# A one-core kernel with a long convolution and a gated MLP: the convolution traced one PSUM tile at a time, its taps on VectorE, its tap gradients as channel products on TensorE, weight tiles of 2 KB per partition

## The chip, the cores and the metric

The kernel runs on one core of one Trainium2 chip. Times are device microseconds (us) of that core, from the start of the program to its end. TensorE (PE) multiplies, VectorE (DVE), ScalarE (ACT) and GpSimd (POOL) do elementwise work, and SyncE (SP) issues the DMAs. Each engine takes its instructions strictly in the order in which they were put into its stream.

## The reference

One block is computed forwards and backwards (S = 2048 rows, D = 1024 channels, F = 3584, bf16 in and out). A small-tap convolution and a 2048-long one run along the rows, channel by channel, beside a gated MLP on the same normalised input:

```python
def _A_ref(q, k, v, shift_k, ssm_k, ssm_D):      # q is xn
    for t in range(4):
        k_shift = k_shift + k_pad[:, t:t + S, :] * shift_k[:, 3 - t][None, None, :]
    kv = k_shift * v
    y = irfft(rfft(kv, 2 * S) * rfft(ssm_k, 2 * S))[:S] + kv * ssm_D
    return q * y
def _B_ref(x, W_gate, W_up, W_down):             # x is xn
    gate = relu(x @ W_gate); h = gate * (x @ W_up)
    return h @ W_down
x = A_q
xn = _layernorm(x, axis=-1)
out = x + _A_ref(xn, A_k, A_v, ...) + _B_ref(xn, B_W_gate, B_W_up, B_W_down)
grads = vjp(...)(grad_out)   # of x, k, v, shift_k, ssm_k, ssm_D, W_gate, W_up, W_down
```

## The kernel before

**The MLP (branch B)** is a run of phases, nearly all of their work matmuls of 128x128 weights on 512 columns. `gate_up` takes 7 blocks `fb` of 512 features, in each 16 row tiles `st`; for one (fb, st) 8 matmuls fill the PSUM tile ps_g and 8 fill ps_u (L585). ACT then makes ru = relu(ps_g) (L600), DVE the gated ps_u (L601), POOL the product ht (L603), and SP stores both to DRAM (ru_d, h_d). `grad_hidden` has 8 matmuls into ps_h per (fb, st), loads ru back (rul), multiplies on DVE (L633) and stores ug_d. `grad_down` (ps_d) and `grad_in` (ps_w) are sums over 16 row tiles (L659), with slabs hs and ugs loaded from DRAM as the streamed operands. `out_phase` (ps_o, L742) and `grad_x` (ps_x, L775) come last. Each of the first four phases has 896 or 1792 such matmuls: gate_up 1792, grad_hidden 896, grad_down 896, grad_in 1792. Weights and slabs use one pool of 6 tiles of [128, 4, 512] (512 KB each).

**The convolution (branch A)** runs over 8 groups of 128 channels. One group is a chain: the small taps of k (`ksh`), the product with v, the transforms of h, g and kv as two matmul steps each (`fwd1`, `fwd2`) with a 32x32 transpose on DVE between them (`flip`, L301), three complex products on DVE (`cmul`: GKV, Y, GH), the inverses (`inv_a`, flip, `inv_b`), and the gradients (`gradients`: gv, gks, and gk by four taps of gks). A PSUM tile of A is 128 partitions by 1024 f32; there are two of them (`aps`), and ACT copies each out (L68). A tap is a POOL product of two halves of 128x1024 (L278) and, from the second tap on, a DVE addition (L72). The gradient of the taps multiplies gks with shifted kp on DVE (`pr`, four of 128x2048 per group) and sums over rows on PE with a selector matrix (`hsel`). Before the gradient taps are complete, gks needs three rows of halo, which come through a small DMA on itself (`gks<-gks`). The tap weights are spread over the partitions by a matmul (`shift_b`, ps_sk).

**What sets the order.** The kernel's Python is traced with priorities (`Pri`): MLP work and A's matmuls and loads are `now`, A's evacuations and stores `late`, and a scheduler lays each engine's instructions out by these. `mlp()` yields after each (fb, st) or 16-matmul sum the time that its matmuls take (3460 ns); when the sum of these has passed 55 us (`A_START`), A's generator `steps()` is advanced: every `yield` in it states how many ns of MLP work are to come before its next piece. A piece is a whole method: all 4 tiles of `fwd1` or of `inv_a`, or 4 tiles of `fwd2`.

Of the kernel before, what the change touches and what calls it, by code (L numbers as in the profile page):

```python
# [17 lines left out]
P = 128  # L18
# [24 lines left out]
class ABranch:  # L43
# [3 lines left out]
    def __init__(self, tc, pri, S, D, k, v, g, shift_k, ssm_k, ssm_D, xn_d, y_d, out_gk, out_gv, out_gsk, out_gh,  # L47
                 out_gsD):
# [54 lines left out]
    def tables(self):  # L103
# [103 lines left out]
        V.memset(self.ones[:], 1.0)  # L207
        V.memset(self.hsel[:], 0.0)
        for i in range(4):
            V.memset(self.hsel[:, i, i:i + 1], 1.0)  # L210
        make_identity(nc, self.identA[:])
        sk_b = con.tile([P, self.NG, 4], BF16, name="sk_b")
        nc.sync.dma_start(out=sk_b[:], in_=self.shift_k.rearrange("(g c) i -> c g i", c=P))
        V.tensor_copy(out=self.skf[:], in_=sk_b[:])
        row = self.ts.tile([1, self.D], BF16, name="sdrow", tag="ts")
        nc.sync.dma_start(out=row[0:1, :], in_=self.ssm_D.rearrange("(o d) -> o d", o=1))
        w = min(1024, self.D)
        psb = self.ps.tile([P, 1024], F32, name="psb", tag="aps")
        for c0 in range(0, w, 512):
            ce = min(w, c0 + 512)  # L220
            nc.tensor.matmul(psb[:, c0:ce], lhsT=self.ones[0:1, :], rhs=row[0:1, c0:ce], start=True, stop=True)
        nc.scalar.copy(out=self.sDb[:], in_=psb[:, 0:w])
# [21 lines left out]
    def loads_2(self, st):  # L244
# [9 lines left out]
        st["kp"], st["vt"] = kp, vt  # L254

    def shift_b(self, st):
        gi = st["gi"]
        dg = self.tmp.tile([P, 4, P], BF16, name="dg", tag="tmp")
        for i in range(4):
            self.pri.late()  # L260
            self.nc.vector.tensor_scalar(out=dg[:, i, :], in0=self.identA[:], scalar1=self.skf[:, gi, i:i + 1],
                                         scalar2=None, op0=ALU.mult)
        ps = self.ps.tile([P, 1024], F32, name="ps_sk", tag="aps")
        self.mm(ps[:, 0:512], self.ones[:], dg[:].rearrange("p i c -> p (i c)"))
        skb = self.sm.tile([P, 4, 1, P], BF16, name="skb")
        self.act(skb[:].rearrange("p i o c -> p (i o c)"), ps[:, 0:512])
        st["skb"] = skb

    def taps(self, st, out, src, offs):

        skb = st["skb"]
        for n, (i, off) in enumerate(offs):
            for hf in range(2):
                rows = slice(off + 8 * hf, off + 8 * hf + 8)
                o = out[:, 8 * hf:8 * hf + 8, :]
                t = o if n == 0 else self.tap.tile([P, 8, P], BF16, name="tap", tag="tap")[:]
                self.pri.late()
# [26 lines left out]
    def fwd1(self, src):  # L304
# [10 lines left out]
        return self.flip(B)  # L315

    def fwd2(self, Bf, form_name, add_D=None):
        F = self.frm.tile([P, 2, 16, P], BF16, name=form_name, tag="frm")
        for k0 in range(0, NB1, 8):
# [5 lines left out]
            re, im = F[rows, 0, kl:kl + 8, :], F[rows, 1, kl:kl + 8, :]  # L325
# [5 lines left out]
        return F  # L331

# [17 lines left out]
    def inv_a(self, Q):  # L350
# [6 lines left out]
        return self.flip(C)  # L357

    def inv_b(self, Cf, dst):
        for j in range(2):  # L360
# [6 lines left out]
            self.act(dst[:, 8 * j:8 * j + 8, :].rearrange("p r c -> p (r c)"), ps[:])  # L367

    def inv_b_chan(self, Cf, dst):
        dv = dst[:, 0:16, :].rearrange("p r c -> p (r c)").rearrange("p (q n) -> p n q", n=NB1)  # L370
        for n0 in range(0, NB1, 16):
# [3 lines left out]
            self.act(dv[:, n0:n0 + 16, :], ps[:])  # L375

    def steps(self):


        nc, pri = self.nc, self.pri  # L380
        nx = self.loads_1(0)
        self.loads_2(nx)
        for gi in range(self.NG):
            st, nx = nx, None
            cg, kp, vt, gt = st["cg"], st["kp"], st["vt"], st["gt"]
            self.shift_b(st)
            hT = self.h_tile(st)
            ksh = self.lng.tile([P, 16, P], BF16, name="ksh")
# [3 lines left out]
            yield 7000  # L392
            Hf = self.fwd1(hT)
            yield 8000
            Gf = self.fwd1(gt)
            yield 8000
            H = self.fwd2(Hf, "H", add_D=self.sDb[:, cg].rearrange("p (o c) -> p o c", o=1))
            if gi + 1 < self.NG:
                nx = self.loads_1(gi + 1)
            yield 8000  # L400
            Kf = self.fwd1(kvt)
            yield 8000
            G = self.fwd2(Gf, "G")
            GKV = self.cmul(H, G, True, "GKV")
            yield 8000
            K = self.fwd2(Kf, "K")
            Y = self.cmul(H, K, False, "Y")
            yield 12000
            Cg = self.inv_a(GKV)
            yield 9000  # L410
            Cy = self.inv_a(Y)
            GH = self.cmul(K, G, True, "GH")
            yield 8000
            gkv = self.ttile("gkv")
            self.inv_b(Cg, gkv)
# [5 lines left out]
            yield 8000
            Ch = self.inv_a(GH)
            yield 5000
            ps = self.ps.tile([P, 1024], F32, name="ps6", tag="aps")
            for i in range(4):
                pr = self.tmp.tile([P, 16, P], BF16, name="pr", tag="tmp")
                self.tt(pr[:], gks[:, 0:16, :], kp[:, 3 - i:19 - i, :], ALU.mult)
                yield 3500
                for j in range(4):
                    self.mm(ps[:, 0:512], self.hsel[:, i, :], pr[:, 4 * j:4 * j + 4, :].rearrange("p r c -> p (r c)"),  # L430
                            start=(i == 0 and j == 0), stop=(i == 3 and j == 3))
            gsf = self.sm.tile([4, P], F32, name="gsf", bufs=1)
            pri.late()
            nc.vector.tensor_reduce(out=gsf[:], in_=ps[0:4, 0:512].rearrange("p (r c) -> p c r", r=4), axis=AX.X,
                                    op=ALU.add)
            self.vcopy(self.gs_all[:, gi, :], gsf[:])
# [25 lines left out]
    def small_outputs(self):  # L462
        nc, NG = self.nc, self.NG
        tp = nc.tensor.transpose
        ps = self.ps.tile([P, 1024], BF16, name="ps7", tag="aps")
        for g in range(NG):
            self.pri.now()
            tp(ps[:, 4 * g:4 * g + 4], self.gs_all[:, g, :], self.identA[0:4, 0:4])
# [17 lines left out]
class LnMlp:  # L486
# [7 lines left out]
    def open_left(self):  # L494
# [18 lines left out]
    def w_tile(self, name):  # L513
        return self.w4.tile([P, 4, 512], BF16, name=name, tag="w4")
# [9 lines left out]

    def layer_norm(self, x, xn_d, xpool, xtag, jpool, jtag, spool):
# [3 lines left out]
        for n in (1, 1, 2, 4, 4, 4):  # L529
            xt = xpool.tile([P, 4, D], BF16, name="ln_x", tag=xtag)  # L530
            nc.sync.dma_start(out=xt[:, 0:n, :], in_=x[st0 * P:(st0 + n) * P, :].rearrange("(t p) d -> p t d", p=P))
# [28 lines left out]
            for j in range(n):  # L560
# [3 lines left out]
                nc.sync.dma_start(out=xn_d[st * P:(st + 1) * P, :], in_=xt[:, j, :])  # L564
# [336 lines left out]
```

## Time and profile before

| | |
|---|---|
| Time, median of 3 runs | 2415.14 us (2412.49 to 2415.37) |
| The profiled execution | 2409.23 us, of which span 2407.4 us |
| PE busy | 2053.3 us, 85% of the span (mean granted clock 0.948) |
| DVE, ACT, POOL busy | 1136.8 us (47%), 722.2 us (30%), 463.1 us (19%) |
| DMA | 352.52 MB, mean 146 GB/s |

A row of a group of waits states for whom an engine stood idle, how long in total, how many times, and the longest. A row of a timeline states start, duration, the instruction with its output and inputs, and in brackets the idle time ahead of it and what ended it. The granted clock is a share of TensorE's full speed. The phases follow one another on PE: first matmul of gate_up at 57.4 us, of grad_hidden at 641.6, of grad_down at 968.7, of grad_in at 1336.0, of out_phase at 1811.6; the last instruction ends at 2407.4.

### The profile page before, as it was taken

What the parts mean: (1) busy time and instruction counts of PE and PEld (TensorE: products, weight loads), DVE (VectorE), ACT (ScalarE), POOL (GpSimd) and SP (SyncE); (2) the same over time, 40 slices, a digit from 0 to 9 for tenths busy, and PEclk for the clock granted to TensorE, in tenths of its full rate; (3) what the DMA queues carried; (4) which work ended last, traced back from release to release, by engine and by line L of the source; (5) the groups of instructions that cost most, each with busy time, mean ns of one, the idle gap of its engine ahead of it and who ended that gap; (6) DMA issues with size and microseconds to landing.
All of it is one profiled execution on the core that took longest, in us unless ns stands there. A gap on an engine that the chain in (4) does not pass through costs nothing.

```text
span 2407.4 us, 26357 instructions
## 1 busy us (share of the span) xinstructions
PE 2053.3 (85%) x10379; PEld 969.4 (40%) x10583; DVE 1136.8 (47%) x1445; ACT 722.2 (30%) x880; POOL 463.1 (19%) x270
## 2 busy tenths in 40 slices
PE   2988689789778858787969688999999899999998
PEld 2434334334334423343424334444444344444443
DVE  6568558557667835386856437300001122232323
ACT  6335335145246422455536236311110000000000
POOL 0342552552530122014150320300000000000000
PEclk9999899899889979898989899999999999999999
DMA  7333433445579867642333521493329975454542
GB/s 232 127 118 108 131 122 110 132 123 145 144 222 271 244 176 242 197 112 73 114 96 120 147 81 62 142 308 109 105 88 220 265 186 138 103 138 101 138 101 70
DMA packets 591166, 352.52 MB, mean 146 GB/s; under 512 B 410817, under 2 KB 530625, under 8 KB 591042
## 3 DMA queue, kind: packets, MB, share of 16 engines
q1 hardware_dynamic: 591042, 350.83, 51.8%
q8 instruction: 83, 1.36, 0.2%
q14 instruction: 41, 0.34, 0.0%
HBM read 154.93 MB, written 124.79 MB: 116 GB/s over the span
## 4 chain that ended last, share of the span: by engine, by line
PE 38%; DVE 8%; DMA 6%; SPq 3%; issue 2%; ACT 2%; POOL 2%; DVEq 0%; ACTq 0%; POOLq 0%
PE ps_x L775 16%; PE ps_w L659 11%; PE ps_o L742 6%; PE ps_d L659 3%; DMA ugs<-ug_d 2%; DVE t L72 2%; DVE flp L301 2%; POOL tap L278 2%; PE ps L64 1%; SPq L734 1%; DVE ksh L72 1%; DVE Y L72 1%; DMA hs<-h_d 1%; ACT G L68 1%; DMA gks<-gks 1%
## 5 line engine op out<-in xcount | busy, mean ns | idle before, releaser
L659 PE MATMUL ps_w<-ugs,xn_nat 128*128 128x512 bf16 x1752 | 401.1, 383 | 20.9 <-DMA ugs<-ug_d 16.5
L585 PE MATMUL ps_u<-wu,xnT 128*128 128x512 bf16 x881 | 230.8, 402 | 82.6 <-DVE ru L601 69.3
L585 PEld LDWEIGHTS <-xnT 128*128 128x128 bf16 x1792 | 177.5, 101 | 300.2 <-issue 115.7
L659 PEld LDWEIGHTS <-xn_nat 128*128 128x128 bf16 x1792 | 175.3, 99 | 233.6 <-issue 34.4
L659 PE MATMUL ps_d<-g_nat,hs 128*128 128x512 bf16 x867 | 222.2, 400 | 28.2 <-DMA hs<-h_d 18.5
L585 PE MATMUL ps_h<-wdT,goT 128*128 128x512 bf16 x872 | 212.4, 396 | 16.8 <-DVE ru L601 9.9
L585 PE MATMUL ps_g<-wg,xnT 128*128 128x512 bf16 x865 | 220.2, 386 | 2.4 <-ACT ru L600 0.5
L603 POOL TENSOR_TENSOR ht<-ru 128x512 bf16<-128x512 bf16 x112 | 151.6, 1358 | 364.0 <-DVE ru L601 274.8
L742 PE MATMUL ps_o<-wd,hT 128*128 128x512 bf16 x878 | 193.3, 379 | 7.6 <-DMA hT<-h_d 6.7
L775 PE MATMUL ps_x<-wuT,guT 128*128 128x512 bf16 x878 | 197.5, 379 | 0.9
L775 PE MATMUL ps_x<-wgT,ggT 128*128 128x512 bf16 x878 | 197.5, 379 | 0.9
L744 DVE TENSOR_TENSOR o<-ps_o,ya 128x512 bf16<-128x512 f32 x32 | 21.4, 687 | 302.4 <-PE ps_o L742 302.2
L695 ACT CAST wi<-ps_w 128x512 bf16<-128x512 f32 x112 | 65.8, 592 | 304.5 <-PE ps_w L659 257.9
L585 PEld LDWEIGHTS <-goT 128*128 128x128 bf16 x896 | 89.9, 101 | 147.1 <-issue 54.8
L600 ACT ACTIVATE ru<-ps_g 128x512 bf16<-128x512 f32 x112 | 68.1, 609 | 245.4 <-PE ps_g L585 159.0
L659 PEld LDWEIGHTS <-hs 128*128 128x128 bf16 x896 | 88.4, 102 | 130.7 <-DMA hs<-h_d 22.1
L633 DVE TENSOR_TENSOR rul<-rul,gh 128x1024 bf16<-128x1024 bf16 x112 | 94.7, 857 | 90.6 <-DMA rul<-ru_d 61.8
L742 PEld LDWEIGHTS <-hT 128*128 128x128 bf16 x896 | 87.4, 98 | 113.3 <-DMA hT<-h_d 8.6
L775 PEld LDWEIGHTS <-guT 128*128 128x128 bf16 x896 | 87.7, 98 | 105.7
L775 PEld LDWEIGHTS <-ggT 128*128 128x128 bf16 x896 | 87.7, 98 | 105.7
L72 DVE TENSOR_TENSOR gk<-gk,tap 128x1024 bf16<-128x1024 bf16 x48 | 74.2, 1568 | 117.0 <-POOL tap L278 117.0
L777 DVE CUSTOM_DVE_ANT_0 gx<-ps_x,gy 128x512 f32<-128x512 f32 x32 | 22.1, 691 | 226.7 <-PE ps_x L775 216.1
(169 smaller groups left out, 2358.3 us busy)
## 6 DMA issues: line engine op xcount, KB each, us to landing
ru_d<-ru SPq DMA_DIRECT2D x112, 256.0 KB, 2.0
rul<-ru_d SPq DMA_DIRECT2D x112, 256.0 KB, 3.9
ug_d<-rul SPq DMA_DIRECT2D x112, 256.0 KB, 3.1
ugs<-ug_d SPq DMA_DIRECT2D x56, 512.0 KB, 5.8
h_d<-ht SPq DMA_DIRECT2D x112, 128.0 KB, 1.7
hs<-h_d SPq DMA_DIRECT2D x28, 512.0 KB, 5.1
out_dram<-wi SPq DMA_DIRECT2D x56, 256.0 KB, 5.4
wg<-in_B_W_gate_dram SPq DMA_DIRECT2D x14, 512.0 KB, 7.4
```

Source lines behind the costliest of these rows:

```text
L64: self.nc.tensor.matmul(out, lhsT=lhsT, rhs=rhs, start=start, stop=stop)
L72: self.nc.vector.tensor_tensor(out=out, in0=in0, in1=in1, op=op)
L278: self.nc.gpsimd.tensor_tensor(out=t, in0=src[:, rows, :], in1=skb[:, i, :, :].to_broadcast([P, 8, P]), op=ALU.mult)
L301: self.nc.vector.transpose(out=df[:, c0:c0 + 32, :], in_=sf[:, c0:c0 + 32, :])
L585: self.nc.tensor.matmul(ps[:], lhsT=xT[:, kt * P:(kt + 1) * P], rhs=w(kt), start=(kt == 0), stop=(kt == self.DT - 1))
L600: nc.scalar.activation(out=ru[:, 0, :], in_=ps_g[:], func=ACT.Relu)
L603: nc.gpsimd.tensor_tensor(out=ht[:], in0=ru[:, 0, :], in1=ru[:, 1, :], op=ALU.mult)
L633: nc.vector.tensor_tensor(out=ru[:], in0=ru[:], in1=gh[:].rearrange("p (o f) -> p o f", o=1).to_broadcast([P, 2, 512]), op=ALU.mult)
L659: self.nc.tensor.matmul(ps[:], lhsT=lhsT(st), rhs=rhs(st), start=(st == 0), stop=(st == self.ST - 1))
L695: nc.scalar.copy(out=wo[:, d, :], in_=ps[:])
L742: nc.tensor.matmul(ps[:], lhsT=hT[:, kt, :], rhs=self.wd[:, kt, oc], start=(kt == 0), stop=(kt == self.FT - 1))
L775: nc.tensor.matmul(ps[:], lhsT=T[:, kt, :], rhs=W[:, kt, oc], start=(i == 0), stop=(i == n - 1))
```

## The change

A's methods `fwd1`, `fwd2`, `inv_a`, `inv_b`, `inv_b_chan` become generators that yield after every PSUM tile, and the MLP yields after every 8 matmuls (1730 ns) where it yielded after 16. Each phase has a pace by which its ns count: 1.0, 0.72, 1.3, 1.3. The taps are DVE products of 128x2048 with the weight broadcast over 16 rows, and DVE additions of the same size; the product ht moves from POOL to DVE. The tap gradients are 16 matmuls gks[r] transposed times kp[r to r+3], 512 columns wide, summed in one PSUM tile, whose four diagonals DVE takes out (a product with the identity and a reduction). The tap weights come from DRAM by a broadcasting load, and `shift_b` goes. In `fwd2` of h ACT evacuates both halves, and D is added once, to 32 rows of the tile B. `inv_b_chan` writes its rows in another order. Weights and slabs become 13 tiles of [128, 2, 512] (256 KB each). In the layer norm all weights of the first block (2 MB) are issued right behind the first chunk of x, and the stores of xn go through POOL's queue.

```diff
     def taps(self, st, out, src, offs):
         skb = st["skb"]
         for n, (i, off) in enumerate(offs):
-            for hf in range(2):
...
-                self.nc.gpsimd.tensor_tensor(out=t, in0=src[:, rows, :], in1=skb[:, i, :, :].to_broadcast([P, 8, P]),
-                                             op=ALU.mult)
-                if n > 0:
-                    self.tt(o, o, t, ALU.add)
+            t = out if n == 0 else self.tmp.tile([P, 16, P], BF16, name="tap", tag="tmp")
+            self.tt(t[:, 0:16, :], src[:, off:off + 16, :], skb[:, i, :, :].to_broadcast([P, 16, P]), ALU.mult)
+            if n > 0:
+                self.tt(out[:, 0:16, :], out[:, 0:16, :], t[:, 0:16, :], ALU.add)
...
+    def grad_taps(self, gi, gks, kp, ns):
+        ps = self.ps.tile([P, 4, P], F32, name="ps6", tag="aps")
+        for r in range(16):
+            self.mm(ps[:].rearrange("p b c -> p (b c)"), gks[:, r, :], kp[:, r:r + 4, :].rearrange("p b c -> p (b c)"),
+                    start=(r == 0), stop=(r == 15))
+            if r % 4 == 3:
...
+                yield ns
...
-            if add_D is not None:
-                self.tt(re, ps[0:64], add_D[0:64].to_broadcast([64, 8, P]), ALU.add)
-            else:
-                self.act(re, ps[0:64])
-            self.act(im, ps[64:128])
+            self.act(F[rows, 0, kl:kl + 8, :], ps[0:64])
+            self.act(F[rows, 1, kl:kl + 8, :], ps[64:128])
+            yield ns
...
-            self.act(dv[:, n0:n0 + 16, :], ps[:])
+            self.act(dv[:, :, n0:n0 + 16], ps[:].rearrange("p n q -> p q n"))
+            yield ns
...
-        return self.w4.tile([P, 4, 512], BF16, name=name, tag="w4")
+        return self.w2.tile([P, 2, 512], BF16, name=name, tag="w2")
...
-                nc.sync.dma_start(out=xn_d[st * P:(st + 1) * P, :], in_=xt[:, j, :])
+                nc.gpsimd.dma_start(out=xn_d[st * P:(st + 1) * P, :], in_=xt[:, j, :])
...
-                nc.gpsimd.tensor_tensor(out=ht[:], in0=ru[:, 0, :], in1=ru[:, 1, :], op=ALU.mult)
+                nc.vector.tensor_tensor(out=ht[:], in0=ru[:, 0, :], in1=ru[:, 1, :], op=ALU.mult)
...
-                yield 3460
+                yield 1730
...
     pri.now()
+    b.ln_load(x, a.frm, "frm", 0)
+    first = b.gate_weights(B_W_gate, B_W_up, 0)
     b.layer_norm(x, xn_d, a.frm, "frm", a.tmp, "tmp", a.sm)
...
+        yield 1.0, b.gate_up(first, B_W_gate, B_W_up, ru_d, h_d)
+        yield 0.72, b.grad_hidden(B_W_down, g, ru_d, ug_d)
+        yield 1.3, b.grad_down(g, h_d, out_9)
+        yield 1.3, b.grad_in(xn_d, ug_d, out_7, out_8)
...
+            left -= ns * pace
```

How the streams move is seen at three places. The first is VectorE in gate_up, where the second group's gradient taps stand. Before, the taps' additions (gk<-gk,tap, in halves) are spread between ru's, each of them behind a POOL product:

```order
L72 TENSOR_TENSOR gks<-gkv,vt 128x2048
L72 TENSOR_TENSOR pr<-gks,kp 128x2048
L601 SCALAR_TENSOR_TENSOR ru<-ru,ps_u 128x512
L72 TENSOR_TENSOR pr<-gks,kp 128x2048
L72 TENSOR_TENSOR gk<-gk,tap 128x1024
L601 SCALAR_TENSOR_TENSOR ru<-ru,ps_u 128x512 x2
L72 TENSOR_TENSOR gk<-gk,tap 128x1024 x2
L601 SCALAR_TENSOR_TENSOR ru<-ru,ps_u 128x512
L72 TENSOR_TENSOR gk<-gk,tap 128x1024 x3
```

In the changed kernel the products stand on the same engine, and ht behind each ru (this is the first group's place):

```order
L72 TENSOR_TENSOR gv<-gkv,ksh 128x2048
L72 TENSOR_TENSOR gks<-gkv,vt 128x2048
L72 TENSOR_TENSOR gk<-gks,skb 128x2048
...
L606 TENSOR_TENSOR ht<-ru 128x512
L604 SCALAR_TENSOR_TENSOR ru<-ru,ps_u 128x512
L606 TENSOR_TENSOR ht<-ru 128x512
L72 TENSOR_TENSOR tap<-gks,skb 128x2048 x2
L72 TENSOR_TENSOR gk<-gk,tap 128x2048
L604 SCALAR_TENSOR_TENSOR ru<-ru,ps_u 128x512
L72 TENSOR_TENSOR gk<-gk,tap 128x2048
```

The `pr` products are gone, and a tap waits for no POOL product; its first product that needs the halo stands behind several ru's.

The second place is ScalarE at the first group's inverse transforms (C is what it copies from a PSUM tile of A). Before, four tiles stand together between ru's:

```order
L68 CAST C<-ps_1809 128x64x16
L68 CAST C<-ps_1819 128x64x16
L68 CAST C<-ps_1829 128x64x16
L68 CAST C<-ps_1839 128x64x16
L600 ACTIVATE ru<-ps_g 128x512 x3
```

After, a ru stands between every two, and PE has 8 MLP matmuls between the matmuls of one tile and of the next:

```order
L68 CAST C<-ps_1818 128x64x16
L68 CAST C<-ps_1843 128x64x16
L603 ACTIVATE ru<-ps_g 128x512
L68 CAST C<-ps_1863 128x64x16
L68 CAST C<-ps_1888 128x64x16
L603 ACTIVATE ru<-ps_g 128x512 x2
```

One tile of A per 8 matmuls of the MLP, where two were filled in a row.

The third place is SyncE around the halo DMA of the group that lies in grad_hidden. Before, it stands amid that phase's own loads and stores:

```order
L628 DMA rul<-ru_d 128x1024 x5
L636 DMA ug_d<-rul 256x1x512 x2
L84 DMA gks<-gks 127x384
L636 DMA ug_d<-rul 256x1x512
L628 DMA rul<-ru_d 128x1024 x2
```

After, it stands behind the whole phase and behind the first loads of the next:

```order
L639 DMA ug_d<-rul 256x1x512
L656 DMA g_nat<-in_grad_out_dram 128x1024 x10
L647 DMA hs<-h_d 128x2x512 x13
L84 DMA gks<-gks 127x384
L84 DMA y_d<-yt 2048x1x128
L683 DMA out_dram<-wo 128x1024
```

On PE this goes with a bare stretch: in the changed kernel A's tiles lie in the first 136 of the 896 ps_h matmuls, and 760 of them have no work of A between them. Counted on PE's stream, 2.74 groups of A then fall into gate_up, 3 into grad_down and 2 into grad_in, whose last 920 ps_w matmuls have none.

## Rows read from the trace of the kernel before

**Rows 1.** Windows by phase: PE, weight loads, DVE, ACT, POOL; clock, DMA, GB/s

```profile
57.40:641.60 584.20, 490.64 (x2589) 234.01 (x2638) 383.14 (x410) 233.18 (x270) 250.02 (x159) 0.94 0.42 125
641.60:968.70 327.10, 245.32 (x1235) 115.74 (x1258) 207.24 (x223) 129.75 (x166) 73.23 (x34) 0.89 0.78 227
968.70:1336.00 367.30, 299.55 (x1688) 146.24 (x1721) 245.90 (x238) 183.97 (x199) 80.55 (x38) 0.91 0.39 115
1336.00:1811.60 475.60, 425.19 (x2111) 197.76 (x2152) 108.02 (x106) 135.75 (x171) 55.30 (x26) 0.97 0.42 130
1811.60:2407.40 595.80, 578.26 (x2636) 262.64 (x2687) 157.54 (x332) 0.58 (x1) 0.00 (x0) 1.00 0.62 147
```

**Rows 2.** Waits of PE: for whom, us in total, times, longest

```profile
PE ps_u L585 <- DVE ru L601: 69.3, 21, 8.7
...
PE ps_d L659 <- DMA hs<-h_d: 18.5, 5, 10.7
PE ps_w L659 <- DMA ugs<-ug_d: 16.5, 13, 4.3
...
PE ps L64 <- ACT C L68: 11.2, 4, 6.5
...
PE ps_d L659 <- DMA g_nat<-in_grad_out_dram: 7.7, 1, 7.7
...
PE ps L64 <- ACT yt L68: 1.3, 3, 0.8
```

**Rows 3.** Waits of VectorE, same columns

```profile
DVE gk L72 <- POOL tap L278: 117.0, 25, 13.5
```

**Rows 4.** Waits of GpSimd, same columns

```profile
POOL tap L278 <- DMA gks<-gks: 70.8, 6, 26.9
```

**Rows 5.** Timeline of VectorE in gate_up, first group's gradient taps

```profile
261.84 3.19 DVE L72 TENSOR_TENSOR gk<-gk,tap 128x1024 bf16<-128x1024 bf16 x2 [10.36 <-POOL tap L278]
```

**Rows 6.** Timeline of PE at the same place

```profile
270.27 3.57 PE L585 MATMUL ps_u<-wu,xnT 128*128 128x512 bf16 x8 [8.60 <-DVE ru L601]
```

**Rows 7.** One window in grad_hidden, columns as in rows 1

```profile
880.00:895.00 15.00, 0.00 (x0) 0.00 (x0) 12.55 (x8) 4.17 (x2) 9.55 (x4) 0.50 0.38 122
```

**Rows 8.** Sum over windows 180 to 240, 360 to 420, 540 to 600

```profile
sum 180.00, PE 162.85 PEld 83.73 DVE 151.55 ACT 100.78 POOL 50.12; mean PE 54.28 PEld 27.91 DVE 50.52 ACT 33.59 POOL 16.71
```

**Rows 9.** One window of out_phase and grad_x, MLP matmuls alone

```profile
1980.00:2040.00 60.00, 59.68 (x274) 27.20 (x278) 12.67 (x25) 0.00 (x0) 0.00 (x0) 1.00 0.52 127
```

**Rows 10.** Timeline of PE: one tile of A's 128-column matmuls

```profile
184.47 0.61 PE L64 MATMUL ps<-flp,FW 128*128 128x128 bf16 x8
184.91 0.59 PE L585 MATMUL ps_u<-wu,xnT 128*128 128x512 bf16 x2
```

**Rows 11.** Line 72, VectorE by form: ns of one, minimum, median, maximum

```profile
L72 DVE TENSOR_TENSOR GKV<-t x64: 673/686/1550, 190.0 to 1472.4; 64x1024 bf16<-64x1024 bf16 x64
...
L72 DVE TENSOR_TENSOR ksh<-ksh,tap x48: 662/1635/2607, 124.3 to 1412.8; 128x1024 bf16<-128x1024 bf16 x48
...
L72 DVE TENSOR_TENSOR H<-ps,sDb x32: 1181/1217/1219, 158.8 to 1450.8; 64x1024 bf16<-64x1024 f32 x32
L72 DVE TENSOR_TENSOR pr<-gks,kp x32: 1199/1226/3149, 240.3 to 1544.9; 128x2048 bf16<-128x2048 bf16 x32
```

**Rows 12.** Line 68, ScalarE by form, same columns

```profile
L68 ACT CAST B<-ps x96: 1012/1018/1072, 125.6 to 1455.1; 128x1024 bf16<-128x1024 f32 x96
...
L68 ACT CAST ghn<-ps x16: 4612/4648/4993, 292.5 to 1556.5; 128x1024 bf16<-128x1024 f32 x16
```

**Rows 13.** Line 601, VectorE by form, same columns

```profile
L601 DVE SCALAR_TENSOR_TENSOR ru<-ru,ps_u x112: 651/680/690, 73.4 to 658.8; 128x512 bf16<-128x512 bf16 x112
```

**Rows 14.** Windows of ps_h's instructions: PE, ACT; granted clock, DMA share, GB/s

```profile
720.00:800.00 80.00, 60.25 (x259) 19.28 (x33) 0.98 0.98 273
937.00:962.00 25.00, 22.66 (x102) 9.36 (x16) 1.00 0.93 303
```

**Rows 15.** The page: what the DMAs moved, in 40 slices of the span

```profile
GB/s 232 127 118 108 131 122 110 132 123 145 144 222 271 244 176 242 197 112 73 114 96 120 147 81 62 142 308 109 105 88 220 265 186 138 103 138 101 138 101 70
```

More of the change, by code (lines that the diff above doesn't have):

```diff
@@ L205, in tables @@
                 V.tensor_scalar(out=o, in0=trB[:], scalar1=mh[:], scalar2=1.0 / 2048, op0=ALU.mult, op1=ALU.mult)
[L207 to L210, printed above, removed]
         make_identity(nc, self.identA[:])
[L212 to L222, printed above, removed]
+        sk_b = con.tile([P, self.NG * 4], BF16, name="sk_b")
+        nc.sync.dma_start(out=sk_b[:].rearrange("c (g i) -> c g i", i=4),
+                          in_=self.shift_k.rearrange("(g c) i -> c g i", c=P))
+        ps = self.ps.tile([self.NG * 4, P], BF16, name="ps_sk", tag="aps")
+        nc.tensor.transpose(ps[:], sk_b[:], self.identA[:])
+        sk_t = con.tile([self.NG * 4, P], BF16, name="sk_t")
+        V.tensor_copy(out=sk_t[:], in_=ps[:])
+        nc.sync.dma_start(out=self.sk_d, in_=sk_t[:])
+        nc.sync.dma_start(out=self.sDb[:], in_=self.ssm_D.partition_broadcast(P))
     def tview(self, ap2d, cg):
@@ L253, in loads_2 @@
         self.load(vt[:], self.tview(self.v, cg))
[L254 to L264, printed above, removed]
         skb = self.sm.tile([P, 4, 1, P], BF16, name="skb")
-        self.act(skb[:].rearrange("p i o c -> p (i o c)"), ps[:, 0:512])
-        st["skb"] = skb
+        self.load(skb[:].rearrange("p i o c -> p (i o c)"),
+                  self.sk_d[4 * st["gi"]:4 * st["gi"] + 4, :].rearrange("i c -> (i c)").partition_broadcast(P))
+        st["kp"], st["vt"], st["skb"] = kp, vt, skb
     def taps(self, st, out, src, offs):
@@ L385, in steps @@
             cg, kp, vt, gt = st["cg"], st["kp"], st["vt"], st["gt"]
-            self.shift_b(st)
             hT = self.h_tile(st)
+            yield 2000
+            yield from self.fwd1(hT, 2000, add_D=self.sDb[:, cg])
+            Hf = self.flipped
             ksh = self.lng.tile([P, 16, P], BF16, name="ksh")
@@ L416, in steps @@
             gks = self.gradients(st, gkv, ksh)
-            yield 8000
+            yield 6000
             yt = self.ttile("yt")
-            self.inv_b(Cy, yt)
+            yield from self.inv_b(Cy, yt, 2000)
             self.store(self.tview(self.y_d, cg), yt[:, 0:16, :])
[L421 to L436, printed above, removed]
+            yield from self.inv_a(GH, 1800)
+            Ch = self.flipped
+            yield from self.grad_taps(gi, gks, kp, 1800)
             if nx is not None:
                 self.loads_2(nx)
+            yield 1500
@@ L439, in steps @@
             ghn = self.ttile("ghn")
-            self.inv_b_chan(Ch, ghn)
+            yield from self.inv_b_chan(Ch, ghn, 2000)
             ghf = ghn[:, 0:16, :].rearrange("p r c -> p (r c)")
@@ L464, in small_outputs @@
         tp = nc.tensor.transpose
[L465 to L468, printed above, removed]
         sk = self.sm.tile([P, NG, 4], BF16, name="sk_o", bufs=1)
-        self.vcopy(sk[:].rearrange("p g i -> p (g i)"), ps[:, 0:4 * NG])
+        self.vcopy(sk[:], self.gs_all[:])
         ps = self.ps.tile([P, 1024], BF16, name="ps8", tag="aps")
@@ L523, in ps_tile, with ln_load @@
         return self.ps.tile([P, 512], F32, name=name, tag="bps")
+    LN_CHUNKS = (1, 1, 2, 4, 4, 4)
+    def ln_load(self, x, xpool, xtag, i):
+        if i >= len(self.LN_CHUNKS):
+            return
+        st0, n = sum(self.LN_CHUNKS[:i]), self.LN_CHUNKS[i]
+        xt = xpool.tile([P, 4, self.D], BF16, name="ln_x", tag=xtag)
+        self.nc.sync.dma_start(out=xt[:, 0:n, :], in_=x[st0 * P:(st0 + n) * P, :].rearrange("(t p) d -> p t d", p=P))
+        self.ln_x.append(xt)
     def layer_norm(self, x, xn_d, xpool, xtag, jpool, jtag, spool):
@@ L528, in layer_norm @@
         st0 = 0
-        for n in (1, 1, 2, 4, 4, 4):
-            xt = xpool.tile([P, 4, D], BF16, name="ln_x", tag=xtag)
-            nc.sync.dma_start(out=xt[:, 0:n, :], in_=x[st0 * P:(st0 + n) * P, :].rearrange("(t p) d -> p t d", p=P))
+        for i in range(1, 5):
+            self.ln_load(x, xpool, xtag, i)
+        for i, n in enumerate(self.LN_CHUNKS):
+            if i == 1:
+                self.ln_load(x, xpool, xtag, 5)
+            xt = self.ln_x[i]
             self.pri.now()
@@ L586, in gemm8, with gate_weights, gate_up @@
                                   stop=(kt == self.DT - 1))
-    def gate_up(self, Wg, Wu, ru_d, h_d):
+    def gate_weights(self, Wg, Wu, fb):
+        return self.col_block(Wg, fb, "wg"), self.col_block(Wu, fb, "wu")
+    def gate_up(self, first, Wg, Wu, ru_d, h_d):
         nc = self.nc
@@ L597, in gate_up @@
                 self.gemm8(ps_g, self.xnT[st], wg)
+                yield 1730
+                self.pri.now()
                 self.gemm8(ps_u, self.xnT[st], wu)
@@ L619, in grad_hidden @@
             wt = []
-            for q in range(2):
+            for q in range(4):
                 t = self.w_tile("wdT")
-                nc.sync.dma_start_transpose(out=t[:], in_=Wd[cols, q * 512:(q + 1) * 512])
+                nc.sync.dma_start_transpose(out=t[:], in_=Wd[cols, q * 256:(q + 1) * 256])
                 wt.append(t)
-            w = lambda kt: wt[kt // 4][:, kt % 4, :]
+            w = lambda kt: wt[kt // 2][:, kt % 2, :]
             for st in range(self.ST):
@@ L851, in mlp @@
     def mlp():
-        yield from b.gate_up(B_W_gate, B_W_up, ru_d, h_d)
-        yield from b.grad_hidden(B_W_down, g, ru_d, ug_d)
-        yield from b.grad_down(g, h_d, out_9)
-        yield from b.grad_in(xn_d, ug_d, out_7, out_8)
+        yield 1.0, b.gate_up(first, B_W_gate, B_W_up, ru_d, h_d)
+        yield 0.72, b.grad_hidden(B_W_down, g, ru_d, ug_d)
+        yield 1.3, b.grad_down(g, h_d, out_9)
+        yield 1.3, b.grad_in(xn_d, ug_d, out_7, out_8)
     a_steps, left = a.steps(), A_START
-    for ns in mlp():
-        left -= ns
-        while a_steps is not None and left <= 0:
-            d = next(a_steps, None)
-            if d is None:
-                a.close()
-                a_steps = None
-                b.open_right(B_W_down)
-            else:
-                left += d
+    for pace, phase in mlp():
+        for ns in phase:
+            left -= ns * pace
+            while a_steps is not None and left <= 0:
+                d = next(a_steps, None)
+                if d is None:
+                    a.close()
+                    a_steps = None
+                    b.open_right(B_W_down)
+                else:
+                    left += d
     b.close_left()
```

124 lines of the change are left out of this document (67 added, 57 removed).

## The prediction

> **What bounds the kernel now.** I read the windows by phase first [rows 1]. From 1811.6 us on PE is busy 578 of 596 us at full clock; the change does not reach it. In the four phases ahead PE is busy 84%, 75%, 82% and 89% at a granted clock of 0.94, 0.89, 0.91 and 0.97, and DMA is dense in grad_hidden alone (0.78). So the loss lies where the convolution is laid between the MLP's matmuls. Next, the price of PE's work at full clock. In a window of pure 512-column matmuls 278 weight loads, one per matmul, go by in 60 us [rows 9]: 0.2158 us each. Eight 128-column matmuls of A take 184.91 - 184.47 = 0.44 us, 0.055 each [rows 10]. A group of A has 56 matmuls of 512 columns (12.1 us), 208 of 128 with the transposes (11.4) and 32 of 64 (about 0.9, at half the price): 24.4 us, 195 for eight groups. The MLP's 1792 + 896 + 896 + 1792 matmuls ahead of 1811.6 us are 1160 us. Together 1355 us of work stand in 1754 us: 399 us are waits, and time at half clock.
>
> Then the waits. PE's largest is for ru on VectorE, 69.3 us in 21 waits [rows 2]; VectorE itself stands 117.0 us for GpSimd's taps before the gk additions [rows 3], and GpSimd 70.8 us for the halo DMA, once 26.9 [rows 4]. One place shows the chain: VectorE idles 10.36 us behind a tap and then adds [rows 5]; the ru queued behind these additions comes late, PE has no free bank for 8.60 us, and the next eight matmuls take 3.57 us [rows 6], where eight at full clock are 1.73. [...]
>
> **The change part by part.**
>
> *Taps.* Removed: the POOL products and the waits on them. A tap's addition takes 662 ns at best and 1635 in the median, per half [rows 11]. Added per group: 14 VectorE operations of 128x2048, 8 products and 6 additions. No row has a product with a weight broadcast over rows; the nearest of that size is pr at 1226 ns, the nearest slow one is H out of PSUM, 1217 for 1024 elements, 2.43 us for 2048 [rows 11]. I take pr's: 17.2 us per group, upper end 8 x 1.21 = 9.7 more. Against this go 12 half additions at 1.64 (19.6), four pr (4.9) and four H halves (4.9). VectorE was busy 245.9 us in grad_down for some 2.6 groups there (821 of its PE instructions are A's, at 313 per group) [rows 1], nearly 95 a group; with 29.4 less, 17.2 more, and 1.3 of the new tap gradients it is 84. *ht* adds 112 operations of 128x512; between a quarter of pr (0.31) and GKV (0.69) I take 0.42, on the line through both rows [rows 11]. In gate_up VectorE then has 112 x (0.68 [rows 13] + 0.42) + 2.74 x 84 = 353 us, of the 487 below. That fits, but not where complex products stand close together.
>
> [...]
>
> *One tile at a time, and H on ScalarE.* A tile is copied out in 1.02 us [rows 12], under the 1.73 of the eight MLP matmuls now between two tiles. So PE's waits on such copies should go: seven rows, from C with 11.2 to yt with 1.3, 39.2 us in all [rows 2], or 2.6% of the 1500 us that A lasts. What then remains? In three stretches of gate_up in which POOL had only ht to do PE was busy 162.9 of 180 us, 9.5% idle [rows 8]. Less 2.6 that is 6.9%: I divide the work of every phase shared with A by 0.931. ghn's strided copy (4.65 us, [rows 12]) is between that and 1.02; it is off the path either way.
>
> *Tap gradients* keep 16 matmuls of 512 columns, so PE is unchanged; VectorE loses pr (counted) and gains two operations of 512 elements, the 1.3 us above (an estimate from H's rate). `shift_b` gives back a matmul a group: nothing.
>
> *2 KB tiles* let a slab's loads start earlier; the hs and ugs waits were 18.5 and 16.5 us [rows 2]. I keep the first whole, since A is denser there, and leave 5 of the second.
>
> *Layer norm.* First matmul at 57.4 us. With 2.1 MB of weights ahead of the second x chunk, at the first slice's 232 GB/s [rows 15], it could come 9 us later; if the weights were what was late, nothing. I take 2.1. [...]
>
> **The sum** (profiled execution):
> - gate_up: (1792 x 0.2158 = 386.7) + 2.74 x 24.4 = 453.6; / 0.931 = 487 (was 584.2).
> - grad_hidden: A lies in the first 17 row tiles only; 33 tiles (by the casts) went by in 80 us with A, 2.42 each, DMA 0.98 busy [rows 14]. The other 95 move 0.59 MB each (two loads or stores of 256 KB, a sixteenth of 1 MB of transposed weights): 1.95 us at the 303 GB/s of the window without transposes, 2.16 at the 273 of that with them [rows 14]; PE's own 1.73 is the floor. I take 2.1: 17 x 2.42 + 95 x 2.1 = 241, and the g_nat wait of 7.7 [rows 2]: 248 (was 327.1).
> - grad_down: 193.4 + 3 x 24.4 = 266.6; / 0.931 = 286; + 18.5 = 305 (was 367.3).
> - grad_in: 872 matmuls and two groups, 237 / 0.931 = 254.5; 920 bare ones, 198.5; + 5 = 458 (was 475.6).
> - the rest 595.8, as before [rows 1].
>
> 59.5 + 487 + 248 + 305 + 458 + 595.8 = 2153; with the 1.8 us outside the span 2155. The median stands 0.245% above the profiled execution (2415.14 to 2409.23): **2160 us**.
>
> **Rivals.**
>
> A, *the waits go entirely*: PE at its work, 57.4 + 454 + 207 + 267 + 436 + 596, about 2025; with half of them gone beyond my sum, 2090. For it: banks (four for the MLP, two for A) cover 3.5 us of lag. Against: VectorE at three quarters, with eight half-products of 0.69 us and their factors in one piece, three times a group.
>
> B, *VectorE becomes the bound*: the broadcast products run at H's rate, 64 x 1.21 = 77 us, all on the path: 2237. For it: VectorE was already busy 84% in the tap-free stretches (151.6 of 180 us [rows 8]), and ht comes on top. Against: pr and the halves run at the fast rate with the same types.
>
> C, *slower*: the chain moves from POOL's queue into VectorE's. gk's later products wait for the halo DMA, and ru is behind them in order. At POOL's worst, 26.9 us [rows 4], in every group, and three times eight matmuls at half clock behind each (1.84 lost each, [rows 6]), that is 32.4 x 8 = 259 us: 2419. It decides from 32 us a group up. Against: POOL's 70.8 us are six waits, so most were near 10, and several ru's now stand between gks and the product that needs the halo.
>
> D, *the change does not spread A*: nothing of A runs under 760 ps_h, and three groups meet in grad_down. Before, that phase took 110 us more than its work (367.3 - 193.4 - 2.6 x 24.4), 92 without hs, 35 a group. At that rate three groups cost 106 in place of my 20: 2247. For it: VectorE's 84 us fall on 89 us of PE's per group. Against: much of the 35 was taps on POOL.
>
> E, *the bare part of grad_hidden is as slow as that with A* (2.42): + 30, 2190.
>
> **How the numbers follow.** My sum 0.56, A 0.12 (half of it near 2090), B 0.10, C 0.04, D 0.12, E 0.06. The likeliest own range is 2115 to 2205. For eight in ten, unknowns ending at half of A and at D: 2090 to 2250. Under 0.2% (about 5 us, what a measurement here can tell from none) counts as the same. Only C reaches that far: faster 0.94, same 0.02, slower 0.04.
>
> **What would show it.** Right: taps of some 1.23 us; no wait of ru on POOL; ps_u's wait on ru far below 69; clock 0.97 or more in gate_up and grad_down; 760 ps_h at 2.1 us per eight with DMA over 0.9; gate_up near 487 and grad_down near 305. Wrong: taps at 2.4; VectorE over 95% in gate_up or grad_down with PE waiting for flips; waits of VectorE on gks of 10 us and more; first ps_g beyond 66 us.

## The result and the profile after

The changed kernel takes 2189.5 us (median of 4 runs, 2184.1 to 2192.7), the kernel before 2414.0 in the same runs: a ratio of 0.907 (0.905 to 0.909). Forecast were 2160, and 2090 to 2250. The profiled execution took 2189.52 us, its span is 2187.8. First the windows by phase, with the columns and cuts of [rows 1] (first matmul of each phase; in the kernel before the first matmuls of grad_in, from 1313.0 us on, already lie amid the last of grad_down, which end at 1335.6):

```profile
61.20:545.20 484.00, 459.68 (x2531) 226.01 (x2579) 347.97 (x490) 225.99 (x272) 2.07 (x5) 0.98 0.51 152
545.20:795.90 250.70, 208.22 (x949) 93.82 (x967) 82.75 (x117) 71.22 (x118) 0.41 (x1) 0.93 0.98 288
795.90:1122.40 326.50, 286.84 (x1768) 145.24 (x1801) 234.84 (x243) 190.11 (x220) 2.48 (x6) 0.97 0.44 122
1122.40:1592.60 470.20, 445.53 (x2343) 214.13 (x2390) 155.58 (x161) 170.30 (x219) 1.24 (x3) 0.97 0.46 141
1592.60:2187.80 595.20, 579.73 (x2635) 263.15 (x2687) 157.40 (x332) 0.58 (x1) 0.00 (x0) 0.99 0.62 147
```

| us | before | forecast | after |
|---|---|---|---|
| up to the first ps_g | 57.4 | 59.5 | 61.2 |
| gate_up | 584.2 | 487 | 484.0 |
| grad_hidden | 327.1 | 248 | 250.7 |
| grad_down | 367.3 | 305 | 326.5 |
| grad_in | 475.6 | 458 | 470.2 |
| the rest | 595.8 | 595.8 | 595.2 |

A hundred us come from gate_up, 76 from grad_hidden. GpSimd's busy time in gate_up falls from 250 to 2 us, and the granted clock rises from 0.94 to 0.98 there, from 0.91 to 0.97 in grad_down. What PE still waits for, whole span, as in [rows 2]:

```profile
PE pst_x L565 <- DVE ln_x L560: 42.0, 6, 10.4
PE ps_h L583 <- DMA wdT<-in_B_W_down_dram: 21.0, 6, 4.6
PE ps L64 <- DVE flp L277: 20.2, 10, 5.2
PE ps_d L662 <- DMA hs<-h_d: 17.0, 1, 17.0
PE ps L64 <- DVE hT L76: 15.3, 4, 7.5
...
PE ps_w L662 <- DMA ugs<-ug_d: 9.5, 6, 3.3
...
PE ps_u L583 <- DVE ru L604: 3.8, 3, 1.4
```

The wait for ru, 69.3 us, has gone to 3.8. VectorE's wait for GpSimd's taps, 117.0 us [rows 3], has no successor; in its place stands the halo DMA (VectorE's waits):

```profile
DVE tap L72 <- DMA gks<-gks: 93.3, 8, 25.4
```

And the tap operations (line 72 by form, ns of one: minimum, median, maximum), against the 1635 of the half additions in [rows 11]:

```profile
L72 DVE TENSOR_TENSOR tap<-kp,skb x24: 1186/1219/1222, 87.3 to 1256.4; 128x2048 bf16<-128x2048 bf16 x24
L72 DVE TENSOR_TENSOR ksh<-ksh,tap x24: 1181/1218/1226, 90.2 to 1257.6; 128x2048 bf16<-128x2048 bf16 x24
```

### The profile page after: what moved, and what is told of

It reads as the page before. It is cut to its first block, busy times and chain, and to the rows that moved or that the text cites. A ratio compares the mean times of both kernels' runs of the same rounds, so it can differ in the third digit from the quotient of the medians.

```text
span 2187.8 us, 26505 instructions
## 1 busy us (share of the span) xinstructions
PE 1996.4 (91%) x10363; PEld 957.0 (44%) x10566; DVE 1013.9 (46%) x1479; ACT 697.2 (32%) x903; POOL 19.3 (1%) x46
## 4 chain that ended last, share of the span: by engine, by line
PE 66%; DVE 12%; DMA 12%; SPq 4%; ACT 3%; issue 3%; POOL 0%; DVEq 0%; ACTq 0%; POOLq 0%
PE ps_x L779 18%; PE ps_w L662 14%; PE ps_o L746 7%; PE ps_u L583 7%; PE ps_g L583 7%; PE ps_h L583 5%; PE ps L64 5%; DMA kp<-in_A_k_dram 2%; DVE flp L277 2%; DVE t L72 2%; PE ps_d L662 2%; DMA gks<-gks 2%; DVE tap L72 2%; DMA ug_d<-rul 2%; ACT G L68 1%
## 5 line engine op out<-in xcount | busy, mean ns | idle before, releaser
L662 PE MATMUL ps_d<-g_nat,hs 128*128 128x512 bf16 x867 | 214.6, 386 | 18.9 <-DMA hs<-h_d 17.0
L583 PE MATMUL ps_u<-wu,xnT 128*128 128x512 bf16 x872 | 215.4, 384 | 17.6 <-DMA wu<-in_B_W_up_dram 11.7
L583 PE MATMUL ps_h<-wdT,goT 128*128 128x512 bf16 x877 | 202.5, 389 | 25.4 <-DMA wdT<-in_B_W_down_dram 21.0
L583 PE MATMUL ps_g<-wg,xnT 128*128 128x512 bf16 x874 | 211.3, 382 | 2.7 <-DVE ru L604 0.9
L636 DVE TENSOR_TENSOR rul<-rul,gh 128x1024 bf16<-128x1024 bf16 x112 | 77.0, 692 | 145.5 <-DMA rul<-ru_d 107.6
L277 DVE STREAM_TRANSPOSE flp<-B 128x1024 f32<-128x1024 f32 x48 | 90.5, 1932 | 71.8 <-ACT B L68 71.8
L635 ACT CAST gh<-ps_h 128x512 bf16<-128x512 f32 x112 | 65.5, 585 | 163.4 <-PE ps_h L583 134.9
```

What stands on the lines that cost most here:

```text
L277: self.nc.vector.transpose(out=df[:, c0:c0 + 32, :], in_=sf[:, c0:c0 + 32, :])
L583: self.nc.tensor.matmul(ps[:], lhsT=xT[:, kt * P:(kt + 1) * P], rhs=w(kt), start=(kt == 0), stop=(kt == self.DT - 1))
L635: nc.scalar.copy(out=gh[:], in_=ps[:])
L636: nc.vector.tensor_tensor(out=ru[:], in0=ru[:], in1=gh[:].rearrange("p (o f) -> p o f", o=1).to_broadcast([P, 2, 512]), op=ALU.mult)
L662: self.nc.tensor.matmul(ps[:], lhsT=lhsT(st), rhs=rhs(st), start=(st == 0), stop=(st == self.ST - 1))
```

## Experiments

Theory 1: the gain is the taps'. Theory 2: it is the one-tile grain and the moving of A. Each kernel below differs from the changed one (2189.5) by what its diff shows, one from the kernel before. Times are medians of 4 runs, of the last kernel a single run; the kernel before took 2414.8 to 2416.3 beside them. Phases are counted from first matmul to first matmul in the profiled execution.

**Taps back on GpSimd.**

```diff
-            self.tt(t[:, 0:16, :], src[:, off:off + 16, :], skb[:, i, :, :].to_broadcast([P, 16, P]), ALU.mult)
+            for hf in range(2):
+                ...
+                self.nc.gpsimd.tensor_tensor(out=t, in0=src[:, rows, :], in1=skb[:, i, :, :].to_broadcast([P, 8, P]),
+                                             op=ALU.mult)
```

> The changed kernel with the taps back as GpSimd products of two halves and VectorE additions; all else as changed. Theory 1 (the gain is the wait for GpSimd that sat in VectorE's queue ahead of ru): VectorE stands some 100 us or more behind taps again, ps_u waits on ru come back to 40 to 70 us, gate_up to 540 us or more, time 2290 to 2340. Theory 2 (the gain is the one-tile grain and the moving of A out of grad_hidden): the waits on GpSimd return on VectorE but PE's banks cover them; gate_up near 500, time 2200 to 2235.

2336.4 us (ratio to before 0.968, 0.966 to 0.970): 147 of the 225 us are lost again, within what theory 1 expected. VectorE stands 156.7 us for the taps before the gk additions and 84.4 before those of ksh. gate_up takes 535 us, grad_hidden and grad_down together 57 more, grad_in 39 more. PE's waits show where:

```profile
PE ps L64 <- DVE flp L282: 64.9, 11, 13.5
PE ps L64 <- DVE hT L76: 62.9, 5, 17.5
...
PE ps_u L588 <- DVE ru L609: 24.6, 6, 6.9
```

The late VectorE hits A's own flips and hT now, more than ru; the 24.6 us for ru are less than the 40 to 70 expected.

**Whole methods as pieces.**

```diff
-            yield from self.fwd1(hT, 2000, add_D=self.sDb[:, cg])
+            yield whole(self.fwd1(hT, 2000, add_D=self.sDb[:, cg]))     # whole: sum(list(gen)); so for every method
...
-                yield 1730
+                yield 3460       # gate_up and gemm16, after 16 matmuls only
```

> The changed kernel with whole methods as pieces again (the ns of a method's tiles summed, the MLP yielding after 16 matmuls); taps stay on VectorE, paces stay. Theory 1 (taps carry the gain): PE's waits on ScalarE's copies return, 30 to 40 us, and nothing else; 2220 to 2235. Theory 2 (the grain carries it): waits on flips and ru grow too, gate_up 530 or more, 2290 and over.

2191.6 us: nothing lost, against both theories. None of PE's waits on ScalarE's copies came back among its larger ones: the largest such row is 3.0 us in all. With taps on GpSimd as well:

> Both of the above at once: taps on GpSimd and whole methods as pieces; what is left of the change are paces, tap gradients on TensorE, ht on VectorE, 256 KB tiles. If the two parts add up, its distance from the changed kernel is the sum of the two single ones. If either alone hides the stalls (banks cover one kind of lateness but not two), it is more than the sum: 2330 or over. By either theory it stays under the kernel before (2414) by what the paces give in grad_hidden, some 50 us.

2329.8 us, 7 less than with the tile grain. So the grain is worth nothing here, with the taps on either engine; neither sum nor "more than the sum" was right.

**Taps alone, in the kernel before** (the 128x2048 VectorE form of the taps in place of the GpSimd halves, nothing else).

> The kernel before with only the taps changed: VectorE products and additions of 128x2048, weights still spread by the matmul. If the taps' 147 us stand by themselves: 2260 to 2275. If they need the rest of the change (the group's pr products and the D additions off VectorE, the moved order): 2300 to 2350.

2269.7 us, ratio 0.939 (0.937 to 0.941): 145 us less. The taps stand by themselves, from either end of the change. gate_up takes 526.3 us here and grad_hidden 261.2: of the 76 us that grad_hidden gains, 66 are there with the taps alone. With the taps on GpSimd and A moved (the first run above) it takes 251.7, so either of the two is enough in that phase. No run puts the paces alone back; what the moving of A is worth by itself is not shown.

**GpSimd busy beside VectorE, nobody waiting.** This asks what it is about GpSimd's taps that costs: the wait for them in VectorE's queue, or that they run at all.

```diff
             self.tt(t[:, 0:16, :], src[:, off:off + 16, :], skb[:, i, :, :].to_broadcast([P, 16, P]), ALU.mult)
+            for hf in range(2):
+                rows = slice(off + 8 * hf, off + 8 * hf + 7)
+                self.pri.late()
+                self.nc.gpsimd.tensor_tensor(out=self.junk[:], in0=src[:, rows, :],
+                                             in1=skb[:, i, :, :].to_broadcast([P, 7, P]), op=ALU.mult)
```

> The changed kernel, and beside VectorE's taps GpSimd makes 16 products of 128x896 per group from the same tiles into a scratch tile that nobody reads (extra work, nothing left out). No engine waits for them. If GpSimd's cost in the kernel before was that its operations beside VectorE's lengthen these: VectorE's 128x2048 operations reach 1.6 us and more on the mean beside them and the time rises by 40 to 80 us. If the cost was the wait in VectorE's queue alone: within 10 us of the changed kernel.

2297.7 us (0.952, 0.949 to 0.954): 108 us more than the changed kernel and more than the 40 to 80 expected, though no engine takes anything from these products. VectorE's waits for the halo and for kp are nearly the same (94.3 and 42.4 us, for 93.3 and 38.6), so that little of it is a wait for GpSimd's queue. VectorE's busy time is 1138.7 us where it was 1013.9. One place in gate_up, first VectorE's timeline, then GpSimd's:

```profile
252.19 2.90 DVE L72 TENSOR_TENSOR tap<-gks,skb 128x2048 bf16<-128x2048 bf16 x1
255.02 2.90 DVE L72 TENSOR_TENSOR gk<-gk,tap 128x2048 bf16<-128x2048 bf16 x1
257.84 0.67 DVE L610 SCALAR_TENSOR_TENSOR ru<-ru,ps_u 128x512 bf16<-128x512 bf16 x1
258.43 2.30 DVE L72 TENSOR_TENSOR gk<-gk,tap 128x2048 bf16<-128x2048 bf16 x1
260.66 0.41 DVE L612 TENSOR_TENSOR ht<-ru 128x512 bf16<-128x512 bf16 x1
260.99 1.21 DVE L72 TENSOR_TENSOR tap<-gks,skb 128x2048 bf16<-128x2048 bf16 x1
```

```profile
251.09 8.56 POOL L260 TENSOR_TENSOR junk<-gks,skb 128x896 bf16<-128x896 bf16 x3 [2.60 <-DMA gks<-gks]
```

While GpSimd runs (251.1 to 259.7 us) an operation of 2048 elements takes 2.90 us; behind its end the same takes 1.21. The ru between them, which reads one operand from PSUM, takes its 0.67 (0.68 on the mean in the changed kernel).

**ht back on GpSimd.**

```diff
-                nc.vector.tensor_tensor(out=ht[:], in0=ru[:, 0, :], in1=ru[:, 1, :], op=ALU.mult)
+                nc.gpsimd.tensor_tensor(out=ht[:], in0=ru[:, 0, :], in1=ru[:, 1, :], op=ALU.mult)
```

> The changed kernel with the product ht back on GpSimd. If VectorE is near its limit in gate_up (0.72 busy, 47 us of it ht): gate_up shorter by 5 to 15 us, 2175 to 2185. If not: the same within 4 us. If GpSimd beside VectorE lengthens VectorE's products of two SBUF operands (the 662 to 1635 ns of the additions before): products of 2048 elements over 1.3 us on the mean, and gate_up longer by 5 us or more.

2209.9 us, 20 more, all in gate_up (505.8 us), by the third expectation. VectorE there is rid of 47 us of ht, and yet its busy time falls by 11 alone. Its groups in gate_up by line (busy us, mean ns), first of the changed kernel, then of this one:

```profile
L277 DVE STREAM_TRANSPOSE flp<-B 128x1024 f32<-128x1024 f32 x18 | 34.3, 1936 | 13.8 <-ACT B L68 13.8
...
L72 DVE TENSOR_TENSOR GKV<-t 64x1024 bf16<-64x1024 bf16 x24 | 16.4, 684 | 0.5
```

```profile
L277 DVE STREAM_TRANSPOSE flp<-B 128x1024 f32<-128x1024 f32 x18 | 34.2, 1935 | 17.9 <-ACT B L68 17.9
...
L72 DVE TENSOR_TENSOR GKV<-t 64x1024 bf16<-64x1024 bf16 x24 | 21.5, 897 | 0.5
```

GKV's operations, of two SBUF operands, are 31% longer on the mean (897 ns for 684), the transposes of B, of one operand, are not (1935 for 1936). PE's wait for ru grows from 3.8 to 14.4 us:

```profile
PE ps_u L583 <- DVE ru L604: 14.4, 13, 2.1
```

**Weight tiles of 512 KB** (6 of [128, 4, 512]; two, two and four loads per block where there are four, four and eight).

> The changed kernel with 6 weight tiles of 512 KB again where it has 13 of 256 KB. If the finer tiles are worth what I gave them (11 us of ugs waits saved, hs unchanged): 2195 to 2205, in grad_in alone. If a slab's loads are hidden anyway: the same within 5 us. If they carry a part of gate_up's gain (wu and wdT waits): gate_up or grad_hidden longer by 10 us or more, 2205 to 2220.

2212.0 us, 22 more, by the third expectation: grad_hidden is 13 us longer, of which the wait for wdT accounts for 5.5 (26.5 us where it was 21.0). grad_in is 7 longer (ugs 18.4 for 9.5), gate_up 2.

**The tap gradients' old VectorE products as extra work** (four `pr` products of 128x2048 per group, unread).

> The changed kernel with the four products gks times shifted kp per group (128x2048, as the kernel before made them for the tap gradients) put back on VectorE as extra work whose result nobody reads: 32 x 1.22 = 39 us of VectorE's time, nothing else. If VectorE has slack everywhere: within 4 us of the changed kernel. If VectorE's queue is what PE waits for in grad_down and in the dense parts of gate_up: 10 to 40 us longer, in those phases, by waits on flips, hT and ru.

2201.2 us, 12 more for 39 us of VectorE's time. gate_up takes nothing of it (483.5 us); grad_hidden and grad_down together take 7 more (222.5 and 361.8 us for 250.7 and 326.5, as the hs wait is gone from the end of the first), grad_in 5, and PE's wait on flips grows:

```profile
PE ps L64 <- DVE flp L277: 33.8, 12, 5.6
```

**The halo DMA, and then all of A's stores, from GpSimd's queue.**

```diff
-        self.store(gks[0:P - 1, 16:19, :], gks[1:P, 0:3, :])
+        nc.gpsimd.dma_start(out=gks[0:P - 1, 16:19, :], in_=gks[1:P, 0:3, :])     # second kernel: in store(), for all
```

> The changed kernel with the halo DMA of gks alone issued from GpSimd's queue, which has nothing else to do. On PE's stream the fourth group then starts under ps_h (200 ps_h before it, 696 beside it) where it stood behind all 896. Theory: the place of that DMA behind SyncE's loads is what kept A out of grad_hidden; VectorE's wait of 93 us on it falls under 30. If grad_hidden has room on PE: grad_down shorter by 20 to 35 us, grad_hidden longer by 5 to 10, time 2165 to 2180. Rival: grad_hidden is bound by DMA (share 0.98), A's loads and stores come on top of it one for one; what grad_down gives back grad_hidden takes, 2185 to 2200.

2175.3 us, ratio to before 0.900 (0.899 to 0.902), 14 less than the changed kernel. The gain lies elsewhere than expected: grad_down is 5.6 us shorter (320.9), not 20 to 35, and grad_in 11.8 (458.4). VectorE's wait:

```profile
DVE tap L72 <- DMA gks<-gks: 24.7, 8, 4.9
```

> The changed kernel with all of A's stores (halo, y, gv, gk, gh) issued from GpSimd's queue. The fourth group lies wholly beside ps_h, the others in grad_down have 424 ps_d each where they had 256 to 305. Theory as for the halo alone, with more: grad_down near its work plus hs (285 to 300), time 2155 to 2175. Rival (grad_hidden bound by DMA): grad_hidden 275 or more, grad_down 300, time 2185 to 2205.

2158.5 us (0.893, 0.891 to 0.895), 31 less. Its windows of grad_hidden, grad_down and grad_in:

```profile
547.20:817.60 270.40, 235.14 (x1224) 112.81 (x1248) 156.73 (x195) 120.45 (x170) 7.94 (x10) 0.96 0.94 268
817.60:1101.80 284.20, 252.33 (x1492) 126.92 (x1519) 161.11 (x167) 140.95 (x168) 11.12 (x15) 0.95 0.48 142
1101.80:1561.90 460.10, 442.32 (x2343) 213.79 (x2391) 154.36 (x159) 169.90 (x219) 11.17 (x15) 0.98 0.47 143
```

grad_hidden, bound by DMA (share 0.94), does get longer by 20 us, but it holds about one more group and the hs wait is gone from its end; with grad_down it is 554.6 us, where it was 577.2. With the paces of grad_down and grad_in at 1.0 besides:

> A's stores on GpSimd's queue, as in the run before that had them there (2158.5), and the paces of grad_down and grad_in at 1.0: groups of 560 matmuls there where they had 424 to 438, 520 bare ps_w at the end where it had 920. If waits in grad_down and grad_in come from A lying dense (VectorE late): 10 to 15 us less, 2143 to 2150. If what is left there are transfers (g_nat, ugs, hT): the same within 5 us.

2145.2 us, ratio to before 0.888 (0.886 to 0.890): the fastest kernel here, 44 us under the changed one. Its grad_down:

```profile
814.70:1075.40 260.70, 239.97 (x1344) 118.05 (x1369) 128.33 (x137) 124.18 (x151) 6.27 (x9) 0.95 0.46 141
```

**xn stores on SyncE's queue again** (a single run).

> The changed kernel with the 16 xn stores on SyncE's queue again; the weights stay ahead of x. Looked at by the first gate_up matmul alone (61.2 us in the changed kernel, 57.4 before). If the stores from GpSimd's queue are late beside VectorE, and that delays PE: 57 to 59. If the 2 MB of weights ahead of x are what delays it: 61 again, or later by the stores that now stand ahead of loads.

First ps_g at 61.8 us, against 61.2: the stores on GpSimd's queue are not what delays it.

## Why the prediction came out as it did

**The taps: right in direction and in their own size.** An operation of 2048 elements takes 1.22 us as pr's row said, with the broadcast operand too (1219 ns in the median), ht 0.42, and rival B (the broadcast at H's rate) is out. That the broadcast would keep pr's time was an estimate from that row alone. What I gave as the cause, the wait for GpSimd in VectorE's queue, is only a part of it: GpSimd's products cost 108 us with nobody waiting for them, against 147 for the real ones. I had the row for it, additions of 662 to 1635 ns [rows 11], and used it as a price, not as a mechanism. The runs show the lengthening: 2.90 us for 1.21 in operations of two SBUF operands beside GpSimd's products, and 0.67 for 0.68 in ru, which reads one operand from PSUM. What brings it about no run shows. How much of the 147 is the wait alone was not separated, since the shadow's products lie beside other operations than the real ones.

**"One tile at a time": this step failed.** I credited it with 2.6% of A's stretch, 39 us. With whole methods as pieces the time is 2191.6 for 2189.5. The waits on ScalarE's copies did go, from 39.2 us to 9.5, but with whole pieces they are 11.5: it was not the grain that removed them. With the taps alone changed, in the kernel before, the same rows still hold 48.2 us, and PE's transposes (pst) wait for ghn besides. The three largest rows there:

```profile
PE ps L64 <- ACT H L68: 17.1, 14, 7.7
PE pst L285 <- ACT ghn L68: 16.0, 5, 3.6
...
PE ps L64 <- ACT ghn L68: 14.3, 5, 3.7
```

So ghn's strided copy was not off the path, as I had it: PE waits 30.3 us for it there. H on ScalarE alone and ghn's new order of writing are the likeliest causes, but neither was put back by itself. Nor did the 39.2 us lie where I took them off: gate_up held 5.5 of them (H 4.5, G and K 0.5 each).

That gate_up came out at 484 for 487 is luck in this term. The 9.5% idle that I read in stretches where GpSimd made only ht [rows 8] held what this ht costs VectorE (GKV 897 ns for 684): with ht on GpSimd the changed kernel's gate_up is 505.8 us, 10.3% of it beyond the work of 453.6; with ht on VectorE it is 6.3%. So ht alone gave 4.0%, where I had taken 2.6 off for the grain. I had entered ht as VectorE work only, 47 us with no gain; it gave 20 us.

**grad_down and grad_in: a term sized too small, by rival D.** The 6.9% of gate_up was carried to grad_down, where three groups lie among 256 to 305 matmuls each; it took 326.5 us for 305, and grad_in 470.2 for 458. These 33.7 us are nearly the whole miss of the span (34.5, the first ps_g being 1.7 late, gate_up 3.0 early, grad_hidden 2.7 late and the rest 0.6 early); the median came out at the profiled execution's own time, so that 29.5 remain. Like for like grad_down missed by more: the 305 held 18.5 us of waits for hs, and the 326.5 hold none, as that wait now lies ahead of the first ps_d. Without it 286 were forecast, 40 us too few, and grad_hidden hid 14 of them. The runs bear out D's mechanism: the halo DMA stood behind grad_hidden's loads on SyncE, as the order rows of SyncE show, and A stood still beside 760 ps_h. With A's stores on the other queue and flat paces grad_hidden, grad_down and grad_in together take 1002.9 us where they took 1047.4, and 1011 were forecast. D's price, 35 us a group, was too high: the 326.5 us are 20 a group beyond the work of 266.6, and 39 with the taps back on GpSimd (382.7 us). How much of the gain is A's spreading was not separated from what SyncE's shorter queue gives: grad_in is 10 to 12 us shorter in both runs with these paces, with as many matmuls (2343) as in the changed kernel.

**Rival C** had the right place, and a price far too high. VectorE waits 93.3 us for the halo, longest 25.4, nearly as feared (waits of 10 us and more were one of my signs of being wrong); taking 69 of these away gave 14 us. In gate_up ru no longer stands directly behind the product that waits (3.8 us of PE waits).

**grad_hidden** came out near its figure, 250.7 for 248, by two misses that cancel. Its matmuls took 233.7 us for 241, bound by DMA (share 0.98), and the hs wait of 17.0 lies ahead of the first ps_d and so in this phase, where I had put a g_nat wait of 7.7.

**2 KB tiles** were worth 22 us, not 11: grad_hidden gained 13 as well, which I had not priced; its waits for wdT show 5.5 of these, and the rest was not followed further.

**The layer norm** lost 3.8 us, inside the bound of 9. The stores are not the cause, as SyncE's queue gives 61.8 us; the weights ahead of x are the likeliest, but were not put back by themselves.

Of the 225 us the taps are 145, and single steps back give ht 20, tiles 22, the pr products 12, the grain 2. The 23 or so that are left (D's additions and ghn's copy among them) were not tried one by one, and single steps need not add.

## What to carry to other kernels

An elementwise operation given to GpSimd was not free here, although GpSimd was idle (108 us with nobody waiting): look at the spread of VectorE's two-operand rows (here 1635 ns in the median, 662 at the least [rows 11]) before taking its cost to be a wait. A small late DMA behind a phase's loads held up a whole side branch here (93.3 us of VectorE's waits), and an idle engine's queue was the place for it (24.7 us of waits, 14 off the time). An idle share read in one stretch holds for the density and the neighbours of that stretch alone.

## What the hardware showed

Beside GpSimd's products VectorE's bf16 operations of 2048 elements with two SBUF operands took up to 2.90 us in place of 1.22 (the kernel with unread products on GpSimd), while ru, with one operand in PSUM, kept its time there (679 ns on the mean, 681 in the changed kernel). With ht on GpSimd the 32x32 transposes of B in gate_up took 1935 ns on the mean, 1936 without; none of the 96 in the kernel before lies wholly beside a product of GpSimd, so what they would take there is not shown. ghn's copy on ScalarE, 4.65 us with strided writes [rows 12], takes 1.01 when it writes runs of 16 contiguous elements and the PSUM read is the strided side:

```profile
L68 ACT CAST ghn<-ps x16: 1007/1012/1019, 259.7 to 1374.1; 128x1024 bf16<-128x1024 f32 x16
```
